# One level of Strassen in the first product of layer two, its operands staged in DRAM

## The chip, the cores and the metric

The kernel runs on one NeuronCore of a Trainium2 chip. The metric is the device time of one execution in microseconds (us), the median of three runs.

## What is computed

```python
# attention with a causal window of 64 positions, per head (4 x 8 heads, 576 positions, 64 wide)
scores = scale * np.matmul(q, k.transpose(0, 1, 3, 2))
mask = (rel >= 0) & (rel < window)
x = attn_out.transpose(0, 2, 1, 3).reshape(B * S, H * D)     # 2304 tokens x 512
# layer one:  w_in 512 x 2048, w_out 2048 x 512
h = x @ w_in;  r = np.maximum(h, 0.0);  x = (s * (r * r) + b) @ w_out
# layer two:  the same sizes, other weights
h = x @ w_in
g = np.maximum(h, 0.0) + alpha * np.minimum(h, 0.0)
out = (g @ w_out).astype(np.float32)
```

The weights of both layers come in as 64-bit floats and are converted on the chip.

## The kernel before, in words

Everything lies transposed: features on the 128 partitions, tokens along the columns. The 512 model features are four slices k of 128, the 2048 hidden features are sixteen tiles f of 128, and the 2304 tokens are five blocks, one of 256 columns and four of 512 (`BLOCKS`, line 24). Each operand of a product is split into a high part (rounded to fp32r) and a low part (what is left), and a product is three passes: high x high, high x low, low x high.

Both layers run the same loop (lines 836 to 850). The tiles f go in groups (`GROUPS`, line 26: five groups in layer one, four groups of four tiles in layer two); for each group all five blocks are gone through. `hidden` (line 638) makes one tile of the hidden layer for one block: 12 matmuls (4 slices k x 3 passes) into one of two PSUM banks `h`, then the activation on ScalarE and VectorE and the split into `gh` and `gl`. In layer two the activation is two Relu steps on ScalarE (lines 692, 693), a multiply-add on VectorE (696), the high part on either engine (701, 702), the low part on VectorE (706). `project` (line 710) multiplies `gh` and `gl` by the tile's w_out: 12 matmuls into four PSUM banks `y0` to `y3`, which `sums` (line 762) adds to SBUF accumulators `ya` at the end of each group and block. In the last group of layer one `sums` also splits the accumulators into the high and low parts of the next layer's x (lines 798 to 807, 20 steps on each of two engines).

`weight` (line 585) loads one tile of 64-bit weights (512 KB, line 597), converts it by two steps on ScalarE (601, 605) and four on VectorE (610, 611, 615, 620) and splits it (624, 629). Attention for a block runs ahead of layer one's first group.

The order of the work is a static one. Every operation is a step with its possible engines, the steps it needs, and a due time `at`; `Plan.emit` (line 134) goes through a list of costs and puts the steps on the engines' queues, first the one that can start first and, between equals, the one due first. On the chip each engine works through its queue in that order and waits on semaphores. All DMAs are issued from SyncE's one queue, also in that order.

## Time and profile before

| | |
|---|---|
| three runs | 877.68, 878.17, 879.06 us, median 878.17 |
| the profiled execution: its span | 876.0 us |
| what lies around the span | no time of its own is given; the median of the runs is 2.2 us above the span |
| TensorE busy | 860.3 us (98%), 5156 matmuls |
| VectorE busy | 567.2 us (65%) |
| ScalarE busy | 397.4 us (45%) |
| moved by DMA | 57.46 MB, mean 66 GB/s |

A busy share is that of the whole span, and the stages differ: attention keeps all engines busy in the first 120 us, and after that TensorE alone is busy throughout. Whether an engine bounds a stage is read from the chain of waits and from what the engine waited for, not from its share.

### The profile page before, as it was taken

Reading aid. Unit: us, or ns where it says so; the run is one execution under the profiler, and the core shown is the slowest. Engines: PE = TensorE matmul, PEld = TensorE weight load, DVE = VectorE, ACT = ScalarE, POOL = GpSimd, SP = SyncE. Lnnn points to the kernel's source line nnn. Section 1 sums busy time; section 2 is a strip of 40 time slices with the busy share of each in tenths; the row PEclk is TensorE's granted clock in tenths of the full one; section 3 lists DMA queues with packets and bytes.
Section 4 is the critical chain, followed back from the end, with each engine's and each line's share of the span. In section 5 each row is a group of like instructions: output and inputs, shape, how many; then the busy total and the mean of one; then the engine's idle time right before and its main releaser. Section 6 shows DMA issues by size and latency. Waiting matters only on the chain.

```text
span 876.0 us, 13000 instructions
## 1 busy us (share of the span) xinstructions
PE 860.3 (98%) x5156; PEld 719.9 (82%) x5156; DVE 567.2 (65%) x985; ACT 397.4 (45%) x909; POOL 53.6 (6%) x73
## 2 busy tenths in 40 slices
PE   7799999999999999999999999999999999999998
PEld 4687788888888888898888888898888888888887
DVE  6988797395477458753788438563687447864444
ACT  6788985352244235332655326442353225522221
POOL 6423330000000000000000000000000000000000
PEclk9999999999999999999999999999999999999999
DMA  8554732031013003200122002120032001201111
GB/s 288 178 172 158 249 92 73 1 88 57 1 48 97 1 4 90 77 25 0 49 73 73 1 1 78 43 73 1 25 96 73 1 1 52 69 0 49 49 49 72
DMA packets 20076, 57.46 MB, mean 66 GB/s; under 512 B 2608, under 2 KB 4656, under 8 KB 20016
## 3 DMA queue, kind: packets, MB, share of 16 engines
q1 hardware_dynamic: 20016, 56.64, 20.1%
q8 instruction: 40, 0.66, 0.3%
q14 instruction: 20, 0.16, 0.1%
HBM read 51.91 MB, written 4.72 MB: 65 GB/s over the span
## 4 chain that ended last, share of the span: by engine, by line
PE 96%; DVE 2%; DMA 1%; POOL 0%; issue 0%; ACT 0%; POOLq 0%; ACTq 0%
PE h L649 45%; PE y L746 41%; PE y L728 4%; PE y L560 2%; PE y L529 2%; PE ab L450 2%; DMA raw<-w_in 1%; DVE nm L475 0%; PE ab L438 0%; DVE wt L620 0%; DVE wt L610 0%; PE y L450 0%; DVE wt L611 0%; POOL yab1.4_706 L507 0%; POOL yab0.4_178 L507 0%
## 5 line engine op out<-in xcount | busy, mean ns | idle before, releaser
L746 PE MATMUL y<-gl,woh 128*128 128x512 f32 (+1 forms) x580 | 181.8, 368 | 0.0
L746 PE MATMUL y<-gh,woh 128*128 128x512 f32 (+1 forms) x580 | 181.8, 368 | 0.0
L746 PE MATMUL y<-gh,wol 128*128 128x512 f32 (+1 forms) x580 | 181.7, 368 | 0.0
L692 ACT ACTIVATE r<-h 128x512 f32<-128x512 f32 (+1 forms) x80 | 44.4, 555 | 225.4 <-PE h L649 225.3
L696 DVE SCALAR_TENSOR_TENSOR r<-qk,nalpha,r 128x512 f32<-128x512 f32 (+1 forms) x80 | 55.7, 696 | 140.1 <-ACT qk L693 139.9
L746 PEld LDWEIGHTS y<-gh,woh 128*128 128x128 f32 x580 | 106.6, 188 | 18.6
L746 PEld LDWEIGHTS y<-gl,woh 128*128 128x128 f32 x580 | 106.5, 188 | 18.4 <-DVE gl L706 0.2
L746 PEld LDWEIGHTS y<-gh,wol 128*128 128x128 f32 x580 | 106.4, 188 | 18.1
L676 DVE SCALAR_TENSOR_TENSOR r<-r,s_sb 128x512 f32<-128x512 f32 (+1 forms) x80 | 58.3, 729 | 80.2 <-ACT r L672 80.0
L672 ACT ACTIVATE r<-h 128x512 f32<-128x512 f32 (+1 forms) x77 | 42.6, 553 | 135.9 <-PE h L649 133.2
L681 ACT ACTIVATE gh<-r,b_sb 128x512 fp32r<-128x512 f32 (+1 forms) x80 | 54.3, 683 | 42.7 <-DVE r L676 40.7
L685 DVE SCALAR_TENSOR_TENSOR gl<-r,b_sb,gh 128x512 fp32r<-128x512 f32 (+1 forms) x80 | 57.2, 717 | 18.8 <-ACT gh L681 18.6
L706 DVE TENSOR_TENSOR gl<-r,gh 128x512 fp32r<-128x512 f32 (+1 forms) x80 | 50.9, 636 | 2.0 <-ACT gh L701 0.4
L615 DVE SCALAR_TENSOR_TENSOR raw<-raw 128x512 int32<-128x512 int32 x64 | 46.1, 727 | 1.4 <-ACT raw L605 1.4
L601 ACT ACTIVATE wt<-raw 128x512 f32<-128x512 f32 x64 | 41.7, 674 | 9.8 <-DMA raw<-w_in 6.4
L605 ACT ACTIVATE raw<-raw 128x512 int32<-128x512 uint32 x64 | 42.4, 678 | 5.5 <-DMA raw<-w_out 2.9
L693 ACT ACTIVATE qk<-h 128x512 f32<-128x512 f32 (+1 forms) x80 | 44.0, 550 | 0.0
L620 DVE CUSTOM_DVE_ANT_0 wt<-raw,wt 128x1024 uint16<-128x1024 uint16 x64 | 43.2, 688 | 0.4
L611 DVE TENSOR_SCALAR wt<-wt 128x512 int32<-128x512 int32 x64 | 28.8, 450 | 2.2
L610 DVE TENSOR_SCALAR wt<-wt 128x512 f32<-128x512 f32 x64 | 28.8, 450 | 0.1
L629 DVE TENSOR_TENSOR wil<-wt,wih 128x512 fp32r<-128x512 f32 x32 | 22.7, 709 | 2.1 <-PE h L649 1.8
L701 ACT CAST gh<-r 128x512 fp32r<-128x512 f32 (+1 forms) x30 | 17.6, 586 | 13.9 <-DVE r L696 13.8
(656 smaller groups left out, 1778.1 us busy)
## 6 DMA issues: line engine op xcount, KB each, us to landing
raw<-w_in SPq DMA_DIRECT2D x32, 512.0 KB, 3.6
raw<-w_out SPq DMA_DIRECT2D x32, 512.0 KB, 4.1
qk<-qk SPq DMA_DIRECT2D x12, 544.0 KB, 3.9
vt<-v SPq DMA_DIRECT2D x8, 256.0 KB, 4.6
qk<-qk SPq DMA_DIRECT2D x4, 512.0 KB, 5.2
vt<-v SPq DMA_DIRECT2D x4, 448.0 KB, 3.4
vt<-v SPq DMA_DIRECT2D x4, 384.0 KB, 4.0
vt<-v SPq DMA_DIRECT2D x4, 320.0 KB, 3.6
```

Source lines behind the costliest of these rows:

```text
L615: [dve(512, lambda: nc.vector.scalar_tensor_tensor(out=L(), in0=H(), scalar=-0x80000000, in1=L(), op0=ALU.bitwise_and, op1=ALU.bitwise_or) ...
L620: [dve(512, lambda: nc.vector.tensor_tensor(ti(), ti(), L(), op=ALU.add), port=True)],
L649: nc.tensor.matmul(T[ps][:, :n], T[w][:, k * P:(k + 1) * P], T[X(x, k)], start=st, stop=sp)
L672: T.step([act(n, lambda: nc.scalar.activation(rn(), hn(), AF.Relu)), dve(n, lambda: nc.vector.tensor_scalar_max(rn(), hn(), 0.0))], reads= ...
L676: [dve(n, lambda: nc.vector.scalar_tensor_tensor(out=rn(), in0=rn(), scalar=s_sb[:, 0:1], in1=rn(), op0=ALU.mult, op1=ALU.mult), port=True)],
L681: [act(n, lambda: nc.scalar.activation(ghn(), rn(), AF.Identity, bias=b_sb[:, 0:1]))],
L685: [dve(n, lambda: nc.vector.scalar_tensor_tensor(out=gln(), in0=rn(), scalar=b_sb[:, 0:1], in1=f32(ghn()), op0=ALU.add, op1=ALU.subtract), ...
L692: T.step([act(n, lambda: nc.scalar.activation(rn(), hn(), AF.Relu))], reads=[ps], writes=[r], at=at - HURRY)
L693: T.step([act(n, lambda: nc.scalar.activation(r2n(), hn(), AF.Relu, scale=-1.0))], reads=[ps], writes=[r2], at=at - HURRY)
L696: [dve(n, lambda: nc.vector.scalar_tensor_tensor(out=rn(), in0=r2n(), scalar=nalpha[:, f:f + 1], in1=rn(), op0=ALU.mult, op1=ALU.add), por ...
L706: [dve(n, lambda: nc.vector.tensor_sub(gln(), rn(), f32(ghn())), port=True)],
L746: nc.tensor.matmul(ps, T[w][:, m * P:(m + 1) * P], T[x][:, :n], start=(i == 0 and j == 0), stop=(last and j == 2),)
```

## The change

Layer two's first product (x by w_in) is no longer made tile by tile but by the seven products of one Strassen step in Winograd's form. A pair p of two tiles f is taken together, and a part q of 768 tokens as two halves of 384 (`HALF`). The 512 model features are two halves of 256. So the block is a 2 x 2 by 2 x 2 product; each of the seven products is 6 matmuls (2 slices of 128 x 3 passes) of 384 columns, 42 for a pair and part in place of 48. Layer two runs over four groups of four tiles, three parts q and two pairs p in each; its second product is as before, in halves of 384 columns.

**The additions between the products** are made in PSUM (`hidden_pair`, line 799 of the changed kernel). Products 1 and 5 open banks `b1` and `b4`; ScalarE copies b1 into a third bank, product 6 is added there by TensorE; that bank is copied into a fourth, products 3 and 7 are added to the third and fourth, the fourth is copied back to `b4`, and product 4 added. VectorE adds product 5 (kept in SBUF) to the third and fourth bank. `lrelu` is the activation of before, at 384 columns, with its results in a ring of ten tiles.

**The operands** are seven pieces of x per part q and seven of w_in per pair. `weight_pair` converts the w_in of layer two during groups two to five of layer one, makes four sums on VectorE, splits the seven pieces and stores them in DRAM (`wd`, 1.84 MB per pair); `weight_load` brings them back, two pairs at a time. `x_pieces` makes the seven pieces of x (four sums of 768 columns on VectorE, seven splits of 768) from layer one's accumulators, one part q after the other, in SBUF for the first part and through two staging places for the others, and stores all in DRAM (`xd`, 0.79 MB per piece); `x_load` brings a part's seven pieces into the seven places X1 to X7, once per group and part.

**Memory**: the separate tiles are replaced by six large areas in which `place` lays the tiles out by hand; a step that writes to a place waits for all users of what lay there. The staging of x, the Relu results and the activations' ring share places.

```diff
+HALF = 384
...
+W2 = 256
+GRING = 10
+LAG = 1.7
+PAIR_AT = (0, 4608)
+W_AT = (3584, 4608, 5632, 6656, 0, 1024)
...
+    def place(self, key, arena, off, cols, dtype=None):
+        live = self.live.setdefault(id(arena), [])
+        end = off + cols
+        old, kept = [], []
...
+        live[:] = kept + [(off, end, key)]
+        assert end <= arena.shape[1]
+        self.tiles[key] = lambda: arena[:, off:end] if dtype is None else arena[:, off:end].bitcast(dtype)
+        self.users[key] = []
+        self.before[key] = sorted(set(old))
+        self.after_alloc[key] = []
+        return key
...
+        def converted(layer, f, part, at, after):
...
+        def pair(cols, src, hi, lo, reads, keys, at, after=0.0, either=True):
+            ways = [act(cols, lambda: nc.scalar.copy(hi(), src()))]
+            if either:
+                ways.append(dve(cols, lambda: nc.vector.tensor_copy(hi(), src()), fast=True))
+            T.step(ways, reads=reads, writes=[k + "h" for k in keys], at=at, after=after)
+            T.step(
+                [dve(cols, lambda: nc.vector.tensor_sub(lo(), src(), f32(hi())), port=True)],
+                reads=reads + [k + "h" for k in keys], writes=[k + "l" for k in keys], at=at, after=after,
+            )
...
+        def weight_pair(n, f1, f2, at, after):
...
+            def adds():
+                nc.vector.tensor_add(sv(0), a(1, 0), a(1, 1))
+                nc.vector.tensor_sub(sv(2), a(0, 0), a(1, 0))
+                nc.vector.tensor_sub(sv(1), sv(0), a(0, 0))
+                nc.vector.tensor_sub(sv(3), a(0, 1), sv(1))
...
+                t = T.place(f"WS{k}.{n}", AQ, (4 * n + k) % 2 * 4 * W2, 2 * cols, F32R)
...
+                pair(cols, s, lambda: v(0), lambda: v(1), reads, [key], at, after)
+                T.step(
+                    dma(1, P * cols * 8, lambda: nc.sync.dma_start(out=wd[n, :, 2 * lo * W2:2 * hi * W2], in_=f32(T[t]))),
+                    reads=[key + "h", key + "l"], writes=[f"wd.{n}.{k}"], at=at + 2, after=after,
+                )
+            stage(0, lambda: x3(T[ts[0]]), [ts[0]])
+            T.step([("dve", 1.75, adds, 0.0, True)], reads=ts, writes=[sums_], at=at, after=after)
+            stage(1, lambda: x3(a(1, 1)), [ts[1]])
+            stage(2, lambda: x3(T[sums_][:, :2 * W2]), [sums_])
...
+        def weight_load(n, at):
+            for k in (0, 2, 3, 1):
+                lo, hi = PIECES[k]
+                w = T.place(f"W{k}.{n}", AW, PAIR_AT[n % 2] + 2 * lo * W2, 2 * (hi - lo) * W2, F32R)
+                T.step(
+                    dma(1, P * (hi - lo) * W2 * 8, lambda w=w, lo=lo, hi=hi: nc.sync.dma_start(
+                        out=f32(T[w]), in_=wd[n, :, 2 * lo * W2:2 * hi * W2])),
...
+        PIECES = ((0, 2), (2, 3), (3, 5), (5, 7))
+        PRODUCTS = {1: (0, 0), 2: (0, 1), 4: (1, 0), 5: (2, 0), 6: (2, 1), 7: (3, 0), 3: (3, 1)}
...
+        def x_slots(g, q, j):
+            return T.place(f"X{j}.{g}.{q}", XA, (j - 1) * XW, XW, F32R)
...
+            def piece(j, s, reads):
+                if direct:
+                    x = x_slots(0, 0, j)
+                elif q < NQ - 1:
+                    x = T.place(f"XS{j}.{q}", *((AQ, 0) if j % 2 else (XA, 7 * XW)), XW, F32R)
+                else:
+                    x = T.place(f"XS{j}.{q}", AG, j % 2 * XW, XW, F32R)
...
+                pair(C, s, lambda: x2(T[x][:, :C]), lambda: x2(T[x][:, C:]), reads, [key], at)
+                T.step(
+                    dma(1, P * XW * 4, lambda: nc.sync.dma_start(out=xd[q, j - 1], in_=f32(T[x]))),
+                    reads=[key + "h", key + "l"], writes=[f"xd.{q}.{j}"], at=at,
+                )
...
+            piece(1, lambda: B(0, 0), src(0, 0))
+            add(1, nc.vector.tensor_sub, lambda: B(0, 1), lambda: B(0, 0), src(0, 0) + src(0, 1))
+            piece(5, tv(1), [temps[1]])
+            add(2, nc.vector.tensor_sub, lambda: B(1, 1), tv(1), src(1, 1) + [temps[1]])
+            piece(6, tv(2), [temps[2]])
+            piece(2, lambda: B(1, 0), src(1, 0))
+            piece(3, lambda: B(1, 1), src(1, 1))
+            add(3, nc.vector.tensor_sub, lambda: B(1, 1), lambda: B(0, 1), src(1, 1) + src(0, 1))
+            piece(7, tv(3), [temps[3]])
+            add(4, nc.vector.tensor_sub, lambda: B(1, 0), tv(2), src(1, 0) + [temps[2]])
+            piece(4, tv(4), [temps[4]])
...
+            T.step(
+                dma(1, P * XW * 4, lambda: nc.sync.dma_start(out=f32(T[x]), in_=xd[q, j - 1])),
+                reads=[f"xd.{q}.{j}"], writes=[key + "h", key + "l"], at=at,
+            )
...
+            b1 = T.tile("b1." + pr, h_ps, [P, 512], F32, "h", 2)
+            b4 = T.tile("b4." + pr, h_ps, [P, 512], F32, "h", 2)
...
+                    for kt in range(2):
+                        for y, (a, c) in enumerate(((0, 0), (0, 1), (1, 0))):
+                            nc.tensor.matmul(
+                                bank(), W[:, a, wj, kt * P:(kt + 1) * P], X[:, c, kt, :],
+                                start=start and kt == 0 and y == 0, stop=kt == 1 and y == 2, skip_group_check=True,
+                            )
...
+            hb2, hb3 = ("hb", 0), ("hb", 1)
+            product(1, 0, b1_, b1, True)
+            product(5, 1, b4_, b4, True)
+            copy(b2_, b1_, [b1], [hb2], 0)
+            copy(lambda: T[p5], b4_, [b4], [p5], 1)
+            product(6, 2, b2_, hb2, False)
+            product(2, 3, b1_, b1, False)
+            copy(b3_, b2_, [hb2], [hb3], 2)
+            product(3, 4, b2_, hb2, False)
+            product(7, 5, b3_, hb3, False)
+            copy(b4_, b3_, [hb3], [b4], 5)
+            product(4, 6, b4_, b4, False)
+            f1, f2 = fs[2 * p], fs[2 * p + 1]
+            lrelu(g, q, 0, 2 * p, f1, b1, b1_, t0 + 3 * slot)
+            lrelu(g, q, 1, 2 * p, f1, *plus("c12", b2_, hb2), t0 + 4 * slot)
+            lrelu(g, q, 1, 2 * p + 1, f2, *plus("c22", b3_, hb3), t0 + 5 * slot)
+            lrelu(g, q, 0, 2 * p + 1, f2, b4, b4_, t0 + 6 * slot)
...
+            G = T.place("g" + key, XA, 7 * XW + g_tile(n, c, i) * 2 * HALF, 2 * HALF, F32R)
...
+            for p in range(2 if g else 0):
+                n = 2 * (g - 1) + p
+                at = begin[0, g, turns(g)[0]] + 30.0 + 40.0 * p - (25.0 if g == len(groups[0]) - 1 else 0.0)
+                weight_pair(n, *groups[1][n // 2][2 * p:2 * p + 2], at, at - 30.0)
...
+            for p in range(2):
+                weight_load(2 * g + p, t + p * PAIR - 10.0)
+            for i, f in enumerate(fs):
+                at = t + LAG * PAIR + i * PAIR / 4 - 12.0
+                weight(1, f, 1, at, at - AHEAD)
+            if g == 0:
+                x_pieces(0, start - 40.0)
+                x_pieces(1, start - 15.0)
+                x_pieces(2, start + 10.0)
+            for q in range(NQ):
+                for p in range(2):
+                    hidden_pair(g, q, p)
+                for c in range(2):
                     for i in range(len(fs)):
-                        hidden(layer, g, bi, i)
-                        project(layer, g, bi, i)
-                    if (layer, g) != (0, 0):
-                        sums(layer, g, bi)
+                        project(1, g, 2 * q + c, i)
...
-    nc = bacc.Bacc("TRN2", target_bir_lowering=False, num_devices=1, dynamic_dma_scratch_size=8192)
+    nc = bacc.Bacc("TRN2", target_bir_lowering=False, num_devices=1, dynamic_dma_scratch_size=1024)
```

Three places show how the queues change. The first is TensorE's queue in the middle of layer two; before (`h` is the bank of the hidden tile, `y` those of the second product):

```order
L649 MATMUL h<-xh0.2_4569,wil_5579 128x512
L649 MATMUL h<-xh1.2_4587,wil_5579 128x512
L649 MATMUL h<-xh2.2_4590,wil_5579 128x512
L649 MATMUL h<-xh3.2_4601,wil_5579 128x512
L746 MATMUL y_6108<-gh,woh_5475 128x512
L746 MATMUL y_6108<-gl,woh_5475 128x512
L746 MATMUL y_6108<-gh,wol_5488 128x512
L746 MATMUL y_6114<-gh,woh_5475 128x512
```

and now (`ax` and `aw` are the areas of x and the weights, `ab` the third and fourth bank; a bare `L824` row of six is one product):

```order
L997 MATMUL y_6799<-ax,wol_6297 128x384
L824 MATMUL ab<-ax,aw 128x384 x6
L997 MATMUL y_6785<-ax,woh_6533 128x384
L997 MATMUL y_6790<-ax,woh_6533 128x384
L997 MATMUL y_6795<-ax,woh_6533 128x384
L997 MATMUL y_6799<-ax,woh_6533 128x384
L997 MATMUL y_6785<-ax,woh_6533 128x384
L997 MATMUL y_6790<-ax,woh_6533 128x384
L997 MATMUL y_6795<-ax,woh_6533 128x384
L997 MATMUL y_6799<-ax,woh_6533 128x384
L824 MATMUL h<-ax,aw 128x384 x6
L997 MATMUL y_6785<-ax,wol_6544 128x384
```

Here product 7 goes into the fourth bank, eight matmuls of the second product follow, then product 4, which needs the copy of the fourth bank, then four more matmuls (the first of them shown), after which the next pair's products 1 and 5 come. Products and second-product matmuls alternate in both, but now a product depends on the one just before it.

The second place is ScalarE's queue in layer two, before (`qk` is the second Relu's result):

```order
L692 ACTIVATE r<-h 128x512
L693 ACTIVATE qk<-h 128x512
L601 ACTIVATE wt<-raw 128x512 x2
L692 ACTIVATE r<-h 128x512
L693 ACTIVATE qk<-h 128x512
L605 ACTIVATE raw<-raw 128x512 x2
L701 CAST gh<-r 128x512
L692 ACTIVATE r<-h 128x512
```

and now:

```order
L835 COPY h<-ab 128x384
L885 CAST ax<-r 128x384
L876 ACTIVATE r<-aq 128x384
L877 ACTIVATE aq<-aq 128x384
L876 ACTIVATE r<-h 128x384
L877 ACTIVATE aq<-h 128x384
L835 COPY ab<-h 128x384
L835 COPY aq<-h 128x384
L835 COPY ab<-ab 128x384
L876 ACTIVATE r<-h 128x384
L877 ACTIVATE aq<-h 128x384
```

The copies between banks (L835) stand between the Relu steps of the earlier tiles, four copies for each pair, one of them (to `aq`) into SBUF.

The third is SyncE's queue at the change from layer one to layer two. Before, there were only weight loads:

```order
L597 DMA raw<-w_in 128x1024
L597 DMA raw<-w_out 128x1024
L597 DMA raw<-w_in 128x1024
L597 DMA raw<-w_out 128x1024
L597 DMA raw<-w_in 128x1024
```

and now (`wd` and `xd` are the pieces in DRAM):

```order
L721 DMA aw<-wd 128x1024
L721 DMA aw<-wd 128x512
L721 DMA aw<-wd 128x1024
L767 DMA xd<-aq 128x1536
L767 DMA xd<-ax 128x1536
L721 DMA aw<-wd 128x1024
L767 DMA xd<-ag 128x1536
L791 DMA ax<-xd 128x1536
L767 DMA xd<-ag 128x1536
L791 DMA ax<-xd 128x1536 x2
L767 DMA xd<-ag 128x1536 x2
L791 DMA ax<-xd 128x1536 x2
```

The loads of the second pair's pieces, the last stores of the second part's pieces of x, the stores of the third part's and the second part's loads follow each other in one queue.

## Rows read from the trace of the kernel before

**Rows 1.** The page: the span, and busy time of TensorE.
```profile
span 876.0 us, 13000 instructions
...
PE 860.3 (98%) x5156; PEld 719.9 (82%) x5156; DVE 567.2 (65%) x985; ACT 397.4 (45%) x909; POOL 53.6 (6%) x73
```
**Rows 2.** The page, the chain that ended last, by engine.
```profile
PE 96%; DVE 2%; DMA 1%; POOL 0%; issue 0%; ACT 0%; POOLq 0%; ACTq 0%
```
**Rows 3.** The chain in order of time: start, length, what, how many.
```profile
176.42 2.72 PE h L649 x12
...
473.49 2.75 PE y L746 x12
...
572.13 2.75 PE y L746 x12
574.88 2.87 PE h L649 x24
```
**Rows 4.** Stretches: length, then busy us (and count) by engine, clock, DMA share, GB/s.
```profile
240.00:315.00 75.00, 75.00 (x370) 63.62 (x369) 48.08 (x82) 28.06 (x49) 0.00 (x0) 1.00 0.15 42
315.00:390.00 75.00, 75.00 (x371) 63.69 (x370) 52.67 (x92) 31.71 (x54) 0.00 (x0) 1.00 0.18 57
390.00:477.00 87.00, 87.00 (x406) 72.88 (x405) 61.31 (x106) 43.70 (x74) 0.00 (x0) 1.00 0.13 43
```
**Rows 5.** Groups by form, ScalarE: shapes, count, busy us, mean ns, idle before.
```profile
L605 ACT ACTIVATE raw<-raw 128x512 int32<-128x512 uint32 x64 | 42.4, 678 | 5.5 <-DMA raw<-w_out 2.9 <-DMA raw<-w_in 2.6
...
L692 ACT ACTIVATE r<-h 128x512 f32<-128x512 f32 x64 | 38.3, 598 | 198.2 <-PE h L649 198.2
...
L692 ACT ACTIVATE r<-h 128x256 f32<-128x256 f32 x16 | 6.1, 384 | 27.2 <-PE h L649 27.1
```
**Rows 6.** Timeline around one hidden tile of layer two: start, length, instruction.
```profile
504.12 0.39 PE L649 MATMUL h<-xh3.1_4402,wil 128*128 128x512 f32 x1
...
504.55 0.60 ACT L692 ACTIVATE r<-h 128x512 f32<-128x512 f32 x1 [6.17 <-PE h L649]
```
**Rows 7.** Groups by form, VectorE.
```profile
L615 DVE SCALAR_TENSOR_TENSOR raw<-raw 128x512 int32<-128x512 int32 x64 | 46.1, 727 | 1.4 <-ACT raw L605 1.4
L706 DVE TENSOR_TENSOR gl<-r,gh 128x512 fp32r<-128x512 f32 x64 | 44.1, 690 | 1.7 <-ACT gh L701 0.4
L620 DVE CUSTOM_DVE_ANT_0 wt<-raw,wt 128x1024 uint16<-128x1024 uint16 x64 | 43.2, 688 | 0.4
...
L611 DVE TENSOR_SCALAR wt<-wt 128x512 int32<-128x512 int32 x64 | 28.8, 450 | 2.2
L610 DVE TENSOR_SCALAR wt<-wt 128x512 f32<-128x512 f32 x64 | 28.8, 450 | 0.1
...
L706 DVE TENSOR_TENSOR gl<-r,gh 128x256 fp32r<-128x256 f32 x16 | 6.8, 422 | 0.3
```
**Rows 8.** DMA issues over the whole span: KB each, median us to landing.
```profile
raw<-w_in SPq DMA_DIRECT2D x32, 512.0 KB, 3.6
...
outT<-ya0.1_5245 SPq DMA_DIRECT2D x1, 256.0 KB, 2.0
...
outT<-ya0.0_5073 SPq DMA_DIRECT2D x1, 128.0 KB, 1.7
```
**Rows 9.** The stretch of the first 22 us, columns as in rows 4.
```profile
0.00:22.00 22.00, 15.68 (x195) 9.70 (x195) 15.21 (x30) 15.22 (x58) 14.22 (x37) 0.92 0.83 289
```
**Rows 10.** DMA issues of the first 22 us alone.
```profile
raw<-w_in SPq DMA_DIRECT2D x3, 512.0 KB, 5.5
```
**Rows 11.** Timeline of the end: last matmul, last addition, last store.
```profile
871.99 0.28 PE L746 MATMUL y<-gh,wol 128*128 128x256 f32 x1
...
872.31 0.42 DVE L787 TENSOR_TENSOR ya3.0_5098<-y,ya3.0_5098 128x256 f32<-128x256 f32 x1
...
873.09 0.40 SPq L794 DMA_DIRECT2D outT<-ya3.0_5098  x1
```

More of the change, by code (lines that the diff above doesn't have):

```diff
@@ L582, in group @@
             return before, after
-        def weight(layer, f, part, at, after):
+        def converted(layer, f, part, at, after):
             key = f"w.{layer}.{f}.{part}"
@@ new lines, in weight @@
+        def weight(layer, f, part, at, after):
+            t = converted(layer, f, part, at, after)
+            key = f"w.{layer}.{f}.{part}"
+            slot = (layer * NF + f) % W_SLOTS[part]
+            if part == 0:
+                hi = T.place(key + "h", AW, W_AT[slot], 512, F32R)
+                lo = T.place(key + "l", AW, W_AT[slot] + 512, 512, F32R)
+            else:
+                hi = T.tile(key + "h", wts, [P, 512], F32R, f"woh{slot}")
+                lo = T.tile(key + "l", wts, [P, 512], F32R, f"wol{slot}")
+            pair(512, lambda: T[t], lambda: T[hi], lambda: T[lo], [t], [key], at, after)
@@ new lines, in lrelu, with x_tile, hidden @@
+                reads=[r], writes=[gh], at=at - HURRY,
+            )
+            T.step(
+                [dve(HALF, lambda: nc.vector.tensor_sub(T[gl], rn(), f32(T[gh])), port=True)],
+                reads=[r, gh], writes=[gl], at=at - HURRY,
+            )
+        lrelu.n = 0
+        def x_tile(k, bi):
+            n = blocks[bi][1]
+            for i, nm in enumerate("hl"):
+                T.place(f"x{nm}{k}.0.{bi}", XA, x_at[bi] + (2 * k + i) * n, n, F32R)
+        def hidden(g, bi, i):
+            n = blocks[bi][1]
+            f = groups[0][g][i]
+            wh, wl = f"w.0.{f}.0h", f"w.0.{f}.0l"
+            key = f"0.{bi}.{f}"
@@ new lines, in hidden @@
+            T.step(
+                [act(n, lambda: nc.scalar.activation(ghn(), rn(), AF.Identity, bias=b_sb[:, 0:1]))],
+                reads=[r, "b"], writes=[gh], at=at - HURRY,
+            )
+            T.step(
+                [dve(n, lambda: nc.vector.scalar_tensor_tensor(
+                    out=gln(), in0=rn(), scalar=b_sb[:, 0:1], in1=f32(ghn()), op0=ALU.add, op1=ALU.subtract), port=True)],
+                reads=[r, gh, "b"], writes=[gl], at=at - HURRY,
+            )
+        hidden.n = 0
```

355 lines of the change are left out of this document (213 added, 142 removed).

## The prediction, made before the change was run

> **What bounds the kernel now.** I read the page's busy times first, then the chain of waits, then stretches, then single forms. The span is 876.0 us and TensorE is busy 98% of it [rows 1]; the chain that ended last runs over TensorE for 96% [rows 2], so what counts is how many matmuls there are, how far apart they start, and whether anything makes them wait. In layer two nothing does. Its chain repeats to the hundredth: the same piece of work starts at 473.49 and at 572.13 us, one group apart [rows 3], so a group lasts 98.64 us and the four 394.6 us. Twelve matmuls of 512 columns take 2.72 us, 0.2267 each; twenty-four of 256 take 2.87 us, 0.1196 each [rows 3]. A group has 384 of the first and 96 of the second: 87.05 + 11.48 = 98.5 us, which is the 98.64 without a gap. In layer one TensorE is busy all of its time too, and VectorE 48 to 53 us of every 75, 61.3 of 87 at the end [rows 4]. Median of the runs and span differ by 2.2 us; I sum against the span and add that. What this measurement can tell from no change is about 0.2%, 1.8 us.
>
> **TensorE's work in layer two.** No row has 384 columns. Between 256 and 512 a column costs (0.2267 - 0.1196)/256 = 0.000418 us, so on a straight line 384 cost 0.1196 + 0.0535 = 0.1731 us. By the column price of 512 alone it would be 0.1700, by that of 256 alone 0.1794; a part per instruction and a part per column lie between, so I take the line. Layer two becomes 1008 + 1152 = 2160 such matmuls: 373.9 us, against 394.6. **Gain 20.7 us** (27 and 7 by the two ends): the 144 matmuls that Strassen leaves out are worth 24.9, and cutting columns by 384 in place of 512 and 256 gives 4.2 back. Two matmuls of 512 columns open the third and fourth bank: +0.45.
>
> **The copies between products.** They are new, on TensorE's path. ScalarE took 0.598 us for 512 columns and 0.384 for 256 [rows 5], so 0.491 for 384. A Relu started 0.43 us after the start of the last matmul it needed [rows 6]; a matmul's place is now 0.173, so that leaves 0.26 behind it. No row shows ScalarE writing a bank, nor TensorE waiting for it; the next instruction after a semaphore in these rows starts within 0.05 to 0.2. Between product 7 and 4 stand eight matmuls, 1.38 us; the copy needs 0.26 + 0.49 + 0.05 = 0.80, so it has 0.6 to spare. Between product 4 and the next pair's product 5, in the same bank, stand ten, 1.73 us; two Relu steps need 0.26 + 0.98 + 0.05 = 1.29, with 0.4 to spare. The other gaps have twelve to eighteen matmuls. Both hold if ScalarE is free. It is not always: its queue is fixed, and a weight step of 0.678 us [rows 5] may stand ahead. Lower bound 0; if one such step stood ahead at both gaps of all 24 pairs, 0.08 + 0.25 each time, 8 us. Weights come in once per group, so I take 3.
>
> **VectorE.** A pair's w_in costs, twice, 0.450 + 0.450 + 0.727 + 0.688 (moved from layer two), then four sums of 256 columns at 0.422 and low parts of 512, 256, 512 and 512 (0.690 or 0.422) [rows 7]: 4.6 + 1.7 + 2.5 = 8.8 us. Two pairs in a group of 75 us put 17.6 on 48 to 53: up to 70 of 75. At the end of layer one two pairs replace four tiles (about +5) and the first two parts of x come in: 14 low parts and 8 sums of 768 columns at 0.690 + 0.268 = 0.958, 21 us plus some casts, against the 20 splits removed (16 of 0.69, 4 of 0.42: 13). So about 61 + 5 + 11 = 77 of 87. It still fits, behind the four buffers of `gh` and `gl`; the cover is thin, though, and what is over is a stall. Lower bound 0; if VectorE needed a tenth more than this in four groups, 70 would become 77 of 75, some 8 us. I take 1. In layer two VectorE loses the w_in steps and gains 48 additions from PSUM of about 0.56; it has room.
>
> **The transfers.** Seven pieces of 0.79 MB per group and part, 5.5 MB, while TensorE makes 180 matmuls, 31.2 us. In the first 22 us the queues moved 289 GB/s [rows 9]; at that rate a part's pieces take 19 us of the 31. A group adds 3.7 MB of weight pieces and 2.1 MB of w_out: 22.3 MB, 77 of 93.5 us at this rate, which was not the ceiling (busy share 0.83). A place X1 to X7 comes free when pair two has used it and is needed by the next part's pair one: by the order of TensorE's queue 13 to 14 us later. A 512 KB load landed after 3.6 us [rows 8], 5.5 in the crowded start [rows 10]; half as many bytes again add 0.9 at 289 GB/s, so 4.5 to 6.4. Hidden, with 7 us to spare. I take 0 for all eleven reloads but those of the handover. In layer one 32 stores of weight pieces, waiting for VectorE's low parts, now stand ahead of later weight loads in SyncE's queue; those loads are due 8 us before their first use and land in 3.6: 0 too, and if they came later, ScalarE's weight steps would. GpSimd's queue is as it was.
>
> **The handover from layer one to layer two.** SyncE's queue loads three blocks of pair two's weights; the third waits for layer one's last hidden tile (call that time 0). Behind it stand two stores of x pieces, whose staging places hold the first Relu results and the first activations. At 289 GB/s: 1.8 us for the load, 2.7 for each store, and about 1.9 more to landing (3.6 - 1.8): the places are free at 6.4 and 9.1. TensorE has eight products and 24 short matmuls to run meanwhile, 11.2 us, then needs an activation that takes a cast, a subtraction and the hops after 9.1, about 1.2: late by nothing to 1.5 us. Next in that queue, stores of the third part's pieces stand ahead of the second part's loads. Counted by TensorE's queue, the place X6 is free at 14.3 us and X3 needed at 26.8. From the one to the other stand a store, two loads, two stores and X3 itself, six transfers of 0.79 MB: 16.3 us at 289 GB/s, 13.6 at what this makes at a full share (289/0.83 = 348), plus 1.9 to landing: 30 to 33, late by 3 to 6, and the pieces to store must come from VectorE in time. The loads behind X3 then have the delay as cover. I take 1 + 3 = 4 us; lower bound 0 (a place may come free earlier), upper bound 12, with 6 late at X3 and a transfer late twice more.
> The Trainium skill's page "DMA: Bandwidth & Descriptors" (section "Latency and other measured facts") speaks against this part: the access time of DRAM, it says, grows from 0.2 us on average to 2 us at high load, and that is most of a transfer's fixed cost. The trace agrees in direction: 5.5 against 3.6 us for the same bytes [rows 10, 8]. By that rule each landing here is up to 1.9 us later, at both spots, the handover costs about 8 in place of 4, and the result would be 4 us higher.
>
> **The ends.** At the start the same loads come in a slightly other order; attention's operations and its places (two of each, as before) are the same: 0, give or take 2. The last block had 256 columns: addition 0.42, store of 128 KB [rows 11]. Now 384 columns: 0.56, and 192 KB, between 1.7 and 2.0 [rows 8]: +0.3.
>
> **Sum.** 876.0 - 20.7 + 0.45 + 3 + 1 + 4 + 0.3 = 864.05; plus 2.2: **866 us**. This case's own range is 860 to 872.
>
> **Rivals.**
> *No stall at all.* Everything hidden: 866 - 8 = 858, give or take attention's 2: 856 to 860. For it: layer two's chain had no gap. Against: there a hidden tile had two banks and nobody waiting.
> *The handover and VectorE eat most of it.* Upper bounds of both, 12 + 8 in place of 5: 881; halfway 874. For it: 70 of 75 us, and one queue for stores and loads. Against: layer one has its four buffers, and the handover comes once. Range 872 to 881, where a dearer matmul would also lead.
> *The chain of products becomes the bound* (slower). Its place is the gaps 7 to 4 and 4 to 5. Without its term of 3 the sum stands 15 us under the time before, so it decides from 15/24 = 0.62 us of stall per pair on. Two weight steps, or other steps as long, ahead of both copies would give 0.8 + 0.9 = 1.7 per pair: 41 us, 904. With half of that, 883. Against it: per pair ScalarE has about 12 steps of 0.49 and two or three casts, some 7.5 of 15.6 us.
> *The reloads become the bound* (slower). If a load only got the rate at which a single one lands, 512 KB in 3.6 us [rows 8], seven pieces would take 39 us of 31: about 7 us for each of 11 reloads, 77 us, 943. The 289 GB/s speak against it.
>
> **How the numbers follow.** Forecast 0.62, no stall 0.09, handover and VectorE 0.13 (half of it still faster by over 0.2%, the rest about even), product chain 0.12, reloads 0.04. Faster by over 0.2% (below 876.4): 0.62 + 0.09 + 0.07 = 0.78. Within 0.2%: 0.06, from the third case's upper part and the chain's lower end. Slower: 0.16. The range 858 to 881 leaves out the lower half of the no-stall case, most of the chain case and the reloads, under 2 in 10.
>
> **What would show it.** Right: groups of layer two 93.5 us apart on the chain, 384-column matmuls 0.173 apart, TensorE's idle time after 130 us a few us and most of it around the handover (near 435 to 470 us), VectorE near 90% in layer one without TensorE waiting, DMA some 160 MB in all. Wrong: TensorE waiting for L835 or L876 in every pair (the chain), for `ax` loads in every part (the reloads), or for `gl` in layer one (VectorE).

## The result, and the profile after

The changed kernel takes **867.14 us**, the median of four runs (864.02 to 867.82), against 878.14 for the kernel before (877.68 to 879.06): a ratio of 0.9868, 95% interval 0.985 to 0.9885. The forecast was 866 with a range of 858 to 881. The profiled execution took 867.01 us with a span of 865.2, 10.8 less than the 876.0 of [rows 1]; the forecast's sum against the span was 864.05. So the total was right within about a microsecond, in part by luck. Its parts were not: two of the small terms came out at nothing (4 us too much in the sum), and two others were larger (some 5 too little).

The page of the kernel after: the span, busy time, what the DMA queues moved, and the chain that ended last (to be held against [rows 1, 2]; before, 57.46 MB were moved in all).
```profile
span 865.2 us, 14218 instructions
...
PE 845.4 (98%) x5398; PEld 763.1 (88%) x5398; DVE 634.9 (73%) x1155; ACT 454.6 (53%) x1057; POOL 52.9 (6%) x73
...
DMA packets 43988, 163.99 MB, mean 190 GB/s; under 512 B 5264, under 2 KB 9872, under 8 KB 43920
...
PE 93%; DVE 3%; ACT 1%; DMA 1%; POOL 1%; issue 0%; POOLq 0%; ACTq 0%; DVEq 0%
```
TensorE still has 98% and its time is 14.9 us shorter, yet the chain lies on it for 93% and no longer 96%: something else sets the time in a few places. The chain in order of time (start, length, what, how many) shows where it doesn't, and one place where it does:
```profile
484.37 2.09 PE ab L824 x12
...
496.20 7.23 DMA xd<-ag
...
537.11 2.08 PE h L824 x12
...
630.71 2.08 PE h L824 x12
```
One group of layer two lies between 537.11 and 630.71: **93.60 us**, where [rows 3] had 98.64. Twelve matmuls of 384 columns take 2.08 us, 0.1733 each; the forecast's straight line gave 0.1731. Four groups are 374.4 us, so 20.2 us less than before; the forecast said 20.7. At 496.20 a store of a piece of x stands on the chain.

Stretches, columns as in [rows 4]: first one of the kernel before, then the kernel after, followed by the waits of TensorE that bear on what comes below (us in total, times, longest):
```profile
22.00:44.00 22.00, 17.12 (x233) 13.71 (x234) 21.37 (x41) 16.42 (x61) 9.23 (x11) 1.00 0.56 179
```
```profile
22.00:44.00 22.00, 18.00 (x218) 13.74 (x219) 20.02 (x38) 14.56 (x54) 8.36 (x10) 0.84 0.49 155
...
240.00:315.00 75.00, 75.00 (x368) 63.51 (x367) 62.05 (x115) 34.27 (x59) 0.00 (x0) 1.00 0.35 120
315.00:390.00 75.00, 75.00 (x345) 62.66 (x344) 61.44 (x110) 38.29 (x64) 0.00 (x0) 1.00 0.45 151
390.00:477.00 87.00, 87.00 (x419) 73.17 (x418) 73.81 (x121) 40.19 (x65) 0.00 (x0) 1.00 0.51 192
...
480.00:520.00 40.00, 35.71 (x196) 34.43 (x196) 30.91 (x55) 22.26 (x48) 0.00 (x0) 0.96 0.87 329
520.00:855.00 335.00, 335.00 (x1933) 334.72 (x1932) 203.29 (x405) 156.15 (x335) 0.00 (x0) 1.00 0.63 226
```
```profile
PE y L564 <- POOL as__89 L547: 6.2, 4, 4.0
PE ab L824 <- ACT ab L835: 2.0, 1, 2.0
...
PE h L912 <- DVE aw L665: 1.6, 1, 1.6
...
PE h L824 <- ACT h L835: 1.1, 1, 1.1
PE h L824 <- ACT aq L877: 1.0, 1, 1.0
```
From 520 to 855 us TensorE is busy 335.00 of 335.00: no copy between products, no reload, no VectorE step makes it wait there. In layer one it is busy all of the time too, with VectorE at 62 of 75 us. It stands still for 4.3 us between 480 and 520, in three waits on ScalarE (L835 twice, L877 once). And in two stretches the granted clock is not 1.00: 0.84 from 22 to 44 us, where the kernel before has 1.00, and 0.96 from 480 to 520. A clock of 0.50 is the lower of the two levels, 1.2 GHz; a value between is the mean of a stretch at both.

**The handover.** TensorE's timeline there (start, length, what; in brackets the wait before it):
```profile
488.64 1.33 PE L824 MATMUL h<-ax,aw 128*128 128x384 f32 x6 [1.15 <-ACT h L835]
...
505.52 1.31 PE L824 MATMUL ab<-ax,aw 128*128 128x384 f32 x6 [2.03 <-ACT ab L835]
506.93 2.02 PE L824 MATMUL h<-ax,aw 128*128 128x384 f32 x6
508.75 2.10 PE L824 MATMUL ab<-ax,aw 128*128 128x384 f32 x6
510.67 1.22 PE L824 MATMUL h<-ax,aw 128*128 128x384 f32 x6
...
512.91 1.32 PE L824 MATMUL h<-ax,aw 128*128 128x384 f32 x6 [1.02 <-ACT aq L877]
```
The three waits make 4.2 us. After the longest, six matmuls take up to 2.1 us in place of 1.2: from 505.52 to 510.67 stand 18 matmuls, 5.15 us where 18 x 0.1733 = 3.12 were due. The granted clock there:
```profile
508.00:510.00 2.00, 2.00 (x7) 2.00 (x7) 1.61 (x4) 1.01 (x3) 0.00 (x0) 0.50 1.00 408
```
So the clock's fall costs 2.0 more. A wait is counted from the end of the matmul before it, and matmuls overlap; counted from start to start, the handover costs a little more than these 6.2. From 484.37 to 514.23 on the chain stand 132 matmuls of 384 columns, 29.9 us where 22.9 were due: **7.0 us**. What the copy at 505 waited for is read backwards through two engines, VectorE's and ScalarE's timelines:
```profile
503.46 0.56 DVE L662 CAST ag<-ay 128x768 fp32r<-128x768 f32 x1 [2.07 <-DMA xd<-ag]
503.93 0.61 DVE L880 SCALAR_TENSOR_TENSOR r<-aq,nalpha,r 128x384 f32<-128x384 f32 x1
```
```profile
504.58 0.51 ACT L885 CAST ax<-r 128x384 fp32r<-128x384 f32 x1 [2.25 <-DVE r L880]
505.00 0.47 ACT L835 COPY ab<-h 128x384 f32<-128x384 f32 x1
```
VectorE's cast for the third part's next piece may not overwrite its staging place before the store that began at 496.20 has landed, 7.23 us later. Behind the cast in VectorE's queue stands an activation step, behind that in ScalarE's a cast, behind that the copy, and TensorE waits for the copy. No load of a piece is late: no wait of TensorE in this run is for `ax<-xd`.

**The balance.** 20.2 us gained on matmuls; 0.45 lost on the two bank openers, 7.0 at the handover; 0.3 gained at the end, where the span stops 3.7 us after the start of the last matmul, before 4.0 [rows 11]. The rest to 10.8 is a loss of 2.2 us ahead of the handover. It is a difference, not a reading; ahead of the handover, the row that differs from before is the one from 22 to 44 us, where the clock fell. The experiments try these two losses, and the terms that came out at nothing.

### The profile page after: what moved, and what is told of

It reads as the page before. It is cut to its first block, busy times and chain, and to the rows that moved or that the text cites. A ratio compares the mean times of both kernels' runs of the same rounds, so it can differ in the third digit from the quotient of the medians.

```text
span 865.2 us, 14218 instructions
## 1 busy us (share of the span) xinstructions
PE 845.4 (98%) x5398; PEld 763.1 (88%) x5398; DVE 634.9 (73%) x1155; ACT 454.6 (53%) x1057; POOL 52.9 (6%) x73
## 4 chain that ended last, share of the span: by engine, by line
PE 93%; DVE 3%; ACT 1%; DMA 1%; POOL 1%; issue 0%; POOLq 0%; ACTq 0%; DVEq 0%
PE y L997 41%; PE h L912 23%; PE h L824 11%; PE ab L824 8%; PE y L979 5%; PE y L595 2%; PE y L564 2%; PE ab L490 2%; ACT as__89 L529 1%; DMA xd<-ag 1%; DVE nm L515 0%; POOL as__89 L547 0%; DVE r L880 0%; DVE ag L665 0%; DVE ax L890 0%
## 5 line engine op out<-in xcount | busy, mean ns | idle before, releaser
L912 PE MATMUL h<-ax,aw 128*128 128x512 f32 (+1 forms) x960 | 216.8, 371 | 2.4 <-DVE aw L665 1.6
L912 PEld LDWEIGHTS h<-ax,aw 128*128 128x128 f32 x960 | 167.0, 188 | 33.2 <-DVE aw L665 1.8
L997 PE MATMUL y<-ax,woh 128*128 128x384 f32 x768 | 172.0, 334 | 0.0
L1032 DVE TENSOR_TENSOR ay<-y,ay 128x384 f32<-128x384 f32 (+2 forms) x152 | 84.8, 594 | 72.0 <-PE y L997 72.0
L997 PEld LDWEIGHTS y<-ax,woh 128*128 128x128 f32 x768 | 136.7, 188 | 0.3 <-DVE ax L890 0.3
L997 PE MATMUL y<-ag,woh 128*128 128x512 f32 (+1 forms) x520 | 135.9, 368 | 0.0
L824 PE MATMUL h<-ax,aw 128*128 128x384 f32 x576 | 113.3, 336 | 2.3 <-ACT h L835 1.1
L997 PEld LDWEIGHTS y<-ag,woh 128*128 128x128 f32 x520 | 93.6, 188 | 16.7
L997 PE MATMUL y<-ax,wol 128*128 128x384 f32 x384 | 105.1, 334 | 0.0
L824 PEld LDWEIGHTS h<-ax,aw 128*128 128x128 f32 x576 | 101.3, 189 | 3.2 <-ACT h L835 1.5
L824 PE MATMUL ab<-ax,aw 128*128 128x384 f32 x432 | 87.2, 337 | 2.0 <-ACT ab L835 2.0
L824 PEld LDWEIGHTS ab<-ax,aw 128*128 128x128 f32 x432 | 76.7, 190 | 2.3 <-ACT ab L835 2.3
```

What stands on the lines that cost most here:

```text
L824: nc.tensor.matmul(bank(), W[:, a, wj, kt * P:(kt + 1) * P], X[:, c, kt, :], start=start and kt == 0 and y == 0, stop=kt == 1 and y == 2, ...
L912: nc.tensor.matmul(T[ps][:, :n], T[w][:, k * P:(k + 1) * P], T[X(x, k)], start=st, stop=sp)
L997: nc.tensor.matmul(ps, T[w][:, m * P:(m + 1) * P], gn(x), start=(i == 0 and j == 0), stop=(last and j == 2),)
L1032: ways = [dve(n, lambda a=a, yn=yn: nc.vector.tensor_add(a(), yn(), a()))]
```

## The experiments

All are edits of the changed kernel. Three things are read in each: the time; the start of the same piece of twelve matmuls, 484.37 in the chain above, as a measure of all that lies before; and what remains from there to the end of the span, as a measure of the handover and layer two.

| kernel | time, us | clock 22 to 44 us | piece starts | from it to the end |
|---|---|---|---|---|
| the change | 867.14 | 0.84 | 484.37 | 380.8 |
| no copies between banks | 866.47 | 0.77 | 486.44 | 378.1 |
| third part later | 864.77 | 0.77 | 486.59 | 377.5 |
| early order of before | 864.22 | 1.00 | 482.36 | 379.0 |
| idle filled | 865.19 | 1.00 | 483.32 | 378.9 |
| both orders | 859.59 | 1.00 | 482.57 | 375.0 |

Times are medians; the other columns come from one profiled execution each, which for "early order", "idle filled" and "both orders" was the fastest of its runs and for "third part later" the slowest. The four runs of the change itself lie between 864.02 and 867.82 us, so a difference of 2 to 3 us between two medians is not clear of the spread; what a single edit does is read from the columns and the waits.

**Six matmuls more per pair: is it TensorE's count?**
```
-                    pe(6, HALF, mms), reads=[w, ...
+                    pe(6, HALF, lambda: [mms() for _ in range(2 if j == 1 else 1)]), reads=[w, ...
```


> Product 1 of every pair is computed twice (the second time opens the bank anew), so TensorE makes 48 matmuls of 384 columns per pair in place of 42, 144 more in all; every other instruction and its order stays. Theory (TensorE's count of matmuls sets layer two): 144 x 0.1733 = 25.0 us longer, 867.1 to 892, and groups 99.8 us apart in place of 93.6. Rival (the pieces' transfers or ScalarE's steps already set the pace of a pair, and TensorE only fills it): 0 to 12 us longer, and waits of TensorE in layer two get shorter by the rest.

Measured: 889.8 us, 22.7 longer (ratio to the kernel before 1.0134, 1.0119 to 1.0149). Groups are 99.84 us apart, as expected; the chain of this kernel:
```profile
539.48 3.12 PE h L824 x18
...
639.32 3.12 PE h L824 x18
```
The 2.3 us that are missing to 25.0 were given back at the handover: the same pieces have more matmuls to hide behind, TensorE idles 1.9 us from 480 to 520 in place of 4.3, and its clock there is 1.00 in place of 0.96 (some of that was lost again early on, where its clock from 22 to 44 us is 0.77). Layer two's pace is TensorE's count.

**No copies between banks.**
```
-                    [act(HALF, lambda: nc.scalar.copy(out(), src()))], ...
+                    [act(HALF, lambda: None if 'hb' in str(reads + writes) else nc.scalar.copy(out(), src()))], ...
-            product(6, 2, b2_, hb2, False)
+            product(6, 2, b2_, hb2, True)
-            product(7, 5, b3_, hb3, False)
+            product(7, 5, b3_, hb3, True)
```


> The 72 copies from one PSUM bank to the next are left out, and products 6 and 7 open their banks anew (so layer two's hidden values lack what the copies carried on); all other instructions stand in the same order. Theory (the copies cost only where layer two begins, where no projections stand between the products): TensorE's waits on L835 of 1.1 and 2.0 us go, the one of 2.0 partly comes back on the next thing behind VectorE; 2 us shorter, between 0 and 4, and the steady groups stay 93.6 us apart. Rival (the copies cost a little in every pair): 24 pairs get shorter by 0.2 us or more each, 5 us or more.

This kernel leaves out what the copies carry on, so its values are not those of the layer; only its time counts. Measured: 866.47 us, 0.7 less than the change, with overlapping ranges (865.1 to 869.0). From the piece to the end it is 2.8 us shorter; before it the clock was lower and took 2.1 back. The steady groups are unchanged. The waits are others, on steps that stand behind the same VectorE:
```profile
PE h L824 <- ACT r L876: 1.7, 1, 1.7
PE h L824 <- ACT aq L877: 1.0, 1, 1.0
PE y L997 <- DVE ax L890: 0.6, 1, 0.6
```
So 72 copies of 0.46 us on TensorE's path cost nothing where projections stand between the products. At the handover the waits without them still make 3.3 us against 4.2, so the copies are for the most part only where lateness is seen first; what else is saved there is the clock's fall, which didn't follow (1.00 from 480 to 520).

**The third part's pieces 20 us later.**
```
-                x_pieces(2, start + 10.0)
+                x_pieces(2, start + 30.0)
```


> One number: the third part's pieces of x are due 20 us later, so that six of the second part's seven loads stand ahead of the third part's stores in SyncE's queue. Theory (VectorE stands still for the store of a staging place, near 501 us, and TensorE behind it): the wait of 2.0 us near 505 us goes, 865 us. Rival (the second part's loads arrive late, which the prediction held for it): the loads come earlier and it goes too, but then a wait on an ax load must be seen in the kernel before this edit, and there is none; so by it nothing changes at 505 us. Third possibility: the third part's casts and differences, moved among the second part's activations, make TensorE wait there: 868 to 871.

Measured: 864.77 us (0.9839, 0.982 to 0.9858), 2.4 less than the change; from the piece to the end 3.3 less. The wait of 2.0 for the copy is gone, and so is the clock's fall after it; the granted clock is 1.00 from 480 to 520. A store of the third part still stands on the chain, later and with 10.25 us, and TensorE waits 1.4 us for VectorE's L841 behind it. So the edit made the wait smaller; that loads arrived late had not been the trouble. It moves the third part's stores behind the loads and its casts behind other steps of VectorE at once, and which of the two did it isn't separated.

**The early order of the kernel before.** The change gave the tile `wt` a third buffer for the pairs of w_in. The planner used it from the first weight on, and the order of ScalarE's and VectorE's steps in the first 40 us changed. Here the planner counts two buffers for the first three tiles:
```
-            t = T.tile("t" + key, wst, [P, 512], F32, "wt", 3)
+            t = T.tile("t" + key, wst, [P, 512], F32, "wt", 3, 2 if layer == 0 and f < 3 else 3)
```


> The third buffer of wt isn't planned for in the first three tiles of layer one, so that the order of the first 40 to 100 us on every engine is again that of the kernel before; everything after is the same kind of work. Theory (the third buffer moved ScalarE's weight steps, TensorE stood idle near 27 and 35 us, and its clock fell to half right after): the granted clock of 22 to 44 us is 1.00 as in the kernel before, 3 us less, 864 us in every run. Rival (the clock's fall hangs on something else than this order, and comes and goes by run): clock 0.99 again in most runs, 867 us.

Measured: 864.22 us (863.16 to 865.51), 2.9 less (0.9844, 0.9829 to 0.9858). The clock of 22 to 44 us is 1.00 and the piece starts 2.0 us earlier, nearly all of the 2.2 of the balance. The other 0.9 of the median cannot be put in one place: from the piece to the end its profiled execution is 1.8 shorter, with 1.4 us in the handover's longest wait where the change had 2.0, and no fall of the clock after it.

**The idle stretches filled with zeros.** That run moves steps as well as the clock, so this one leaves every step where it is.
```
+                    for _ in range((5, 3)[h] if gi == 5 else 0):
+                        nc.tensor.matmul(Q_(h), idle[:, :P], idle, start=True, stop=True)
...
+                for _ in range(12 if (g, bi, i) == (0, 0, 1) and which[0][0] == wl else 0):
+                    nc.tensor.matmul(T[ps][:, :n], idle[:, :P], idle[:, :n], start=False, stop=False)
```


> The kernel with the change, with 20 matmuls of zeros in TensorE's queue where it stood idle: twelve of 256 columns that add zero ahead of the low products of the second tile (1.56 us of waiting near 28.7 us), five and three of 512 ahead of the transposes that waited 1.2 and 0.8 us near 35 us (their bank is written anew after). Nothing else is moved, and VectorE's, ScalarE's, GpSimd's and SyncE's queues are the same. Theory (the idle stretches are what the clock's fall follows): granted clock of 22 to 44 us 1.00, or 0.95 and more, in place of 0.84, and 2 to 3 us shorter, 864 to 865. Rival (the clock's fall has another cause, or a fixed place): 0.84 or lower again, and 867 to 868.

Measured: 865.19 us (864.04 to 865.33), 2.0 less, with 20 matmuls more. In stretches of 2 us, the kernel after and then the one with the zeros:
```profile
26.00:28.00 2.00, 0.92 (x7) 0.45 (x5) 1.97 (x4) 1.17 (x2) 0.39 (x1) 1.00 0.77 268
30.00:32.00 2.00, 2.00 (x26) 1.20 (x23) 1.30 (x4) 2.00 (x9) 0.00 (x0) 0.50 0.00 0
36.00:38.00 2.00, 1.53 (x8) 1.01 (x8) 1.97 (x6) 0.68 (x3) 0.15 (x1) 0.56 0.34 137
38.00:40.00 2.00, 2.00 (x31) 1.93 (x32) 1.00 (x3) 2.00 (x13) 0.00 (x0) 0.59 0.03 8
```
```profile
26.00:28.00 2.00, 1.74 (x16) 1.48 (x15) 1.97 (x3) 1.35 (x3) 1.30 (x2) 1.00 0.90 285
30.00:32.00 2.00, 1.41 (x36) 1.24 (x35) 1.97 (x5) 2.00 (x13) 0.00 (x0) 1.00 0.00 0
36.00:38.00 2.00, 1.44 (x17) 0.94 (x18) 1.97 (x6) 1.14 (x5) 0.28 (x1) 1.00 0.38 152
38.00:40.00 2.00, 2.00 (x37) 1.93 (x33) 1.98 (x5) 2.00 (x13) 0.00 (x0) 1.00 0.35 27
```
TensorE was busy 0.92 us of the two from 26 to 28, and a little later ran at 0.50; with zeros in that place it is at 1.00 throughout. So at the same order of all steps the fall went with the idle time. One profiled execution each doesn't prove it: the fall comes and goes with the same order. One of the change's four runs had a mean clock of 0.998, as the kernel before has, and a run further below with the same steps and no zeros up to the handover (the same bytes without that wait) had these rows:
```profile
0.00:22.00 22.00, 16.18 (x194) 10.51 (x194) 14.93 (x29) 14.51 (x52) 14.43 (x39) 0.84 0.78 275
26.00:28.00 2.00, 2.00 (x16) 1.73 (x16) 1.97 (x3) 1.58 (x4) 1.46 (x2) 1.00 0.72 246
```
There the clock was lower earlier (0.84 in the first 22 us, 0.92 in [rows 9]), TensorE was busy all of the time from 26 to 28, and from 22 to 44 it ran at 1.00. That fits idle time as what the fall follows. Yet its piece starts at 484.22, hardly earlier than the change's, so the clock from 22 to 44 us isn't the whole of the loss: with the zeros the piece starts 1.1 us earlier, with the early order 2.0. The profiled execution with zeros is 3.0 us shorter in all; the other 1.9 are again a shorter wait at the handover, after which the clock stayed up, and the edit doesn't explain them.

**Both orders together.** The two one-line edits, early order and third part later.

> The early order of the kernel before together with the third part's pieces due 20 us later. Theory (two separate losses, 3 us of clock near 30 to 40 us and 2.4 us of waiting near 500 us): both gains add up, 861.8 us, granted clock 1.00 in 22 to 44 us and TensorE idle under 2 us from 480 to 520. Rival (the planner moves so much around the handover with each edit that the second gain is chance): one of the two only, 864 us.

Measured: **859.59 us** (859.35 to 860.63; 0.979, 0.9777 to 0.9804), 7.5 less than the change and 18.7 less than the kernel before, which took 878.25 beside it. Its clock and idle time:
```profile
22.00:44.00 22.00, 16.99 (x234) 13.40 (x233) 21.12 (x41) 17.00 (x63) 9.33 (x12) 1.00 0.58 182
480.00:520.00 40.00, 39.48 (x230) 38.85 (x229) 31.58 (x56) 24.01 (x54) 0.00 (x0) 1.00 0.75 284
```
Most of both losses is gone and the gains are more than their sum (861.8 expected): 1.8 us before the piece, 5.8 from it to the end, of the handover's 7.0. In the run with the third part later a wait of 1.4 us for L841 had been left; here it is 0.2. Why, wasn't tried; the planner orders the second group of steps anew with each edit.

**And layer two due 6 us earlier.**
```
+    now -= 6.0
     NQ = NT // (2 * HALF)
```


> As the last one, and layer two is due 6 us earlier, so that the first pair's products stand between the last projections of layer one instead of close behind each other. Theory (what is left of TensorE's idle time at the handover, 1.8 us, is the first pair's copies and activations with nothing between the products): 0.5 to 1.8 us less, 860 to 861.3. Rival (the pieces of part two come later relative to layer two then, and their loads become the wait): 861.8 or more, with a wait for ax.

Measured: 860.31 us (859.59 to 860.44). No gain: TensorE idles 1.4 us from 480 to 520 where 0.5 were left, in new waits of 0.8 for L877 and 0.6 for L842 (841 in the other kernels).

**Every load of a piece twice.**
```
+                ... lambda: [nc.sync.dma_start(out=f32(T[x]), in_=xd[q, j - 1]) for _ in range(1 if g == 0 else 2)]), ...
```


> Every load of a piece of x in groups two to four of layer two is issued twice in a row, to the same place: 63 more transfers of 0.79 MB, all else as it was. A part's 7 loads become 14, while TensorE still makes 31.2 us of work on it. Theory (a place is free 13 to 14 us before it is needed, a load lands in 6.1 us, so some 7 us are to spare for each): a second load costs 2.3 to 2.7 us more to landing, and TensorE still waits little; at 348 GB/s 14 loads take 31.6 us, so 0 to 8 us longer in all nine parts, 867 to 875. Rival (the loads were only just hidden): 2.5 us and more of wait in every one of the nine parts, 20 to 60 us longer, with waits for ax loads at the head of each part.

Measured: 1068.0 us, 201 longer, far outside both. The waits of SyncE's queue say why it is no measure of the margin:
```profile
SPq L791 <- DMA ax<-xd: 331.5, 63, 6.5
```
Each second load to the same place waited for the first to land, 5.3 us on average, 63 times, so 14 transfers that should overlap stood one behind the other. Not all of the 201 us is waiting: from 520 to 1055 us TensorE stands still for 133, and its matmuls take 402 at a mean clock of 0.85 where 335 were due, 67 more. The run shows something else: the rival in which a load gets only the rate of a single one is real when the queue waits for each landing. In the change it doesn't.

**The same bytes without that wait.**
```
+                nc.sync.dma_start(out=xe[(g - 1) * NQ + q, j - 1], in_=xd[q, j - 1])
```


> Behind each load of a piece of x in groups two to four stands one more transfer of the same 0.79 MB, from DRAM to a DRAM place of its own that nothing reads, so that, unlike in the run with every load twice, no transfer waits for the landing of another; all else is as it was. Per part 7 transfers become 14, 11 MB. Theory (there the wait of SyncE for each landing cost the 201 us, and the bytes alone would fit): at 348 GB/s 14 take 31.6 us of the 31.2 of a part, 0 to 8 us longer in all nine parts, 867 to 875. Rival (the rate of the queues is used up, 244 GB/s on the mean of layer two): the nine parts wait by what the added 50 MB take beyond the free time, 60 us and more longer.

Measured: 885.77 us (1.0084, 1.007 to 1.0098), 18.6 longer, 2.1 for each of the nine parts. From 700 to 850 us the queues moved 386 GB/s at a busy share of 0.95, and a load of a piece landed after 11.3 us (the second row, from 610 to 860 us, 372 GB/s on the mean):
```profile
700.00:850.00 150.00, 142.70 (x815) 140.61 (x814) 86.30 (x174) 62.15 (x134) 0.00 (x0) 1.00 0.95 386
```
```profile
ax<-xd SPq DMA_DIRECT2D x49, 768.0 KB, 11.3
```
An estimate from it: a group of these carries 38.8 MB (the forecast's 22.3 and 21 x 0.79), 100.5 us at 386 GB/s against 93.6 of matmuls: 21 us in three groups. TensorE's longest waits behind 520 us are for `ax<-xd` (7.9 us) and for the copy into `h` (5.7). So the bytes set the time here, and the cost is neither 0 to 8 nor 60. The change itself moves 226 GB/s with a landing of 6.1 us; at 386, 93.6 us would carry 36 MB, so by this estimate there is room for some 60% more bytes.

**VectorE in layer one, loaded further.** The four sums of a pair four times over, then twice:
```
-            T.step([("dve", 1.75, adds, 0.0, True)], ...
+            T.step([("dve", 1.75, lambda: [adds() for _ in range(4)], 0.0, True)], ...
```


> The four sums of each pair of w_in tiles are made four times over: 3 x 1.68 = 5.0 us more of VectorE per pair, 40 us in all, 10 us in a layer-one group of 75 us where it was busy 62; the order of everything else stays. Theory (VectorE has the rest of its time free and hidden tiles have four buffers behind them): TensorE doesn't wait in layer one, 867 us, 0 to 2 us longer. Rival (the prediction's lower margin: VectorE's fixed order has no room, and 5 us in one piece are too long for the buffers): 2 to 5 us of wait per pair for gh or gl, 16 us and more longer, 883 or above.

> The four sums of each pair of w_in tiles twice over, where an earlier run had them four times and lost 13.5 us: 1.68 us more of VectorE per pair, 13.4 in all. Theory (VectorE's room in layer one ends somewhere between 62 and 72 us of 75: the added time is free until then): 867 to 868. Rival (VectorE's steps stand in the way at once, a third of what is added is lost): 4.5 us longer, 871.6.

Measured: four times 880.63 us, 13.5 longer, between the two (0 to 2 by the theory, 16 and more by the rival); twice 867.89, 0.8 longer, which is no difference beside the change's own spread. With four times, TensorE waits where VectorE is busy 64 to 68 us of 75:
```profile
240.00:315.00 75.00, 71.55 (x333) 59.49 (x332) 64.01 (x126) 32.88 (x55) 0.00 (x0) 0.98 0.33 113
315.00:390.00 75.00, 72.53 (x338) 60.63 (x337) 67.83 (x133) 32.76 (x56) 0.00 (x0) 0.98 0.39 128
```
So 13.4 us of VectorE more are free in layer one, and 40 cost a third of themselves, although VectorE then is not yet full. That a fixed order can't use all of its idle time would explain it; no run tries another order.

## Why the prediction was right, and where it wasn't

*TensorE's work* (20.7): right, 20.2, by 0.1733 per matmul and a group of 93.60. It is the term that decided the sign, and the only one whose price came from two rows of the same operation.

*The copies between products* (3): mis-sized; 0 in the steady groups. (Between the end of one instruction and the start of the one that waits for it [rows 6, 11] show 0.04 and 0.36 us, not "0.05 to 0.2"; the sums used 0.05.) The forecast doubted whether ScalarE would be free at the gaps; TensorE is busy 335.00 of 335.00 us, so it was, at each of the pairs in that stretch. The row that bears on it was ScalarE's low load, which the text gave as an argument against the rival and then didn't use for the term.

*VectorE* (1, at 70 of 75 and 77 of 87): 0, at 62 and 73.8. The 17.6 us for two pairs were added to 48 and to 52.67 alike, though these stretches converted six and eight tiles of weights, and both convert ten now; and the mean durations of [rows 7] are of the whole run, 0.727 and 0.45 us, against 0.686 and 0.43 in these stretches. The warning about a thin cover was sound: 10 us more per group cost 13.5 us in all.

*The transfers* (0): right. Landings of 6.1 us stand in the forecast's 4.5 to 6.4, and at 386 GB/s the rate did exceed 348.

*The handover* (1 + 3): 7.0, by another way than predicted, and at 484 to 514 us, not "near 435 to 470". The failed step is "from the one to the other stand a store, two loads, two stores and X3 itself ... late by 3 to 6": no load was late. The same queue of stores and loads was late for whoever produces the pieces. The forecast asked that "the pieces to store must come from VectorE in time", and did not ask what VectorE's queue holds behind a piece that may not be written yet: activations, and behind them the copies. The waits of 1.1 and 1.0 us are for a copy and an activation at places with no projections between the products. The page "DMA: Bandwidth & Descriptors" of the Trainium skill (section "Latency and other measured facts") has the access time of DRAM grow with load. The trace agrees in direction: stores of the same size landed after 3.7 us in layer one's last stretch (the median of `xd<-ax`) and after 7.23 on the chain; the queues moved 192 GB/s there and 329 from 480 to 520 us. By that rule the forecast would have had 8 for this place; 7.0 were measured, of which 2.0 are clock, and no load was waited for.

*Attention and the ends* (0, give or take 2, and +0.3): the end -0.3, the start 2.2 by the balance and 2.0 by the early order, at the edge of its bound. The failed step is "attention's operations and its places (two of each, as before) are the same": they were, but their order was not, because the third buffer of `wt` let ScalarE's weight steps move. The order of ScalarE's and VectorE's first steps would have shown this before the run.

So the total came out because 4 us too much for copies and VectorE stood against 3 too little for the handover and 2 for the start; that is luck, and the gain on matmuls is not.

Of the rivals, none came true. The first, no stall at all (856 to 860), is what the kernel with both orders does: 859.59. The reloads as the bound had the wrong price, yet the run with every load twice shows its mechanism where the queue waits for each landing.

## What to carry to other kernels

When a store frees a staging place, ask what stands behind the instruction that fills the place again, on its engine and on the next ones: the wait travels along fixed queues until it reaches the engine that sets the time. A buffer added for one stage can reorder another that shares it; compare each engine's order at places that the change doesn't mean to touch. And count a stall of TensorE with the slow matmuls that may follow it.

## What the runs showed of the hardware that was not expected

TensorE's clock fell after short waits in the middle of dense work: after the 2.03 us at the handover twelve matmuls ran at about half pace, which made that wait twice as dear. It fell after waits of 2.2 us there too (the sums four times and twice), and not after 1.4 (early order), 1.6 (idle filled) and 1.7 (no copies); whether the length of the wait is what decides it, no run tries. From 22 to 44 us the mean clock of the same early order was 0.84 in some profiled executions, 0.77 in others and 1.00 in one, and one of the change's four runs, with a mean of 0.998 over the span in place of 0.992 to 0.994, took 864.02 us: some 3 us of the spread between runs go with this clock. With twenty matmuls of zeros the median is 2 us lower.

A load of 0.79 MB landed after 6.1 us (median) where the queues moved 226 GB/s, and after 11.3 at 372, with the same number of places to fill.
